# Four batches of attention and a two-stage mixture: the first batch's attention and transform rebuilt, the second batch's queued behind the first unit

## The chip, the cores and the metric

The kernel runs on one NeuronCore of a Trainium2 chip. The metric is device time in microseconds (us): the time of one execution on that core, as a median of three runs.

## The reference, cut to what matters

Three modules in a row, on 4 batches (b) of 576 positions and 512 features (8 heads of 64):

```python
# attention, for each batch and head
qd, kd, vd = mean over groups of 4 positions of q, k, v          # 144 positions
low   = softmax(qd @ kd.T / 8) @ vd, each row repeated 4 times
local = softmax(where(|i - j| < 4, q @ k.T / 8, -1e9)) @ v
x = low + local
# transform, layernorm and MLP
u  = x + real(fft(fft(x, over positions), over features))
x2 = u + relu(layernorm(u) @ w1) @ w2                            # 512 -> 2048 -> 512
# gate, value and output
gate = sigmoid(causal convolution of x2 over 5 positions, one filter per feature)
out  = (gate * (x2 @ w_val)) @ w_out
```

## The kernel before

**Layout.** Activations lie transposed: X is four tiles of 128 features by 584 positions, for one batch. TensorE (PE) multiplies, VectorE (DVE), ScalarE (ACT) and GpSimd (POOL) do the rest, SyncE (SP) issues the loads one behind another (`load`).

**Attention of a batch** (`attn_steps`). The local part goes in five blocks of some 115 query positions, each for two sets of heads (passes): scores dS on PE (L470, L476), their row maximum dmx on DVE, the exponent dP on ACT, row sums dsu and the division on DVE or GpSimd, then transposes dPT (L511) and the values dO (L522), both on PE. The low-resolution part runs beside it: sums over four positions (qkT, L529), scores sc, exponent E, transposes eT, values po (L650) and `base`, which is added to X. For the pooled v (vr) the first batch has six PE products with a matrix of zeros and ones, c_pool; the later batches have adds on GpSimd.

**Transform** (second half of `attn_steps`). Cosines and sines come as products. fs and fF (L698, L706) are sums and differences of X with its mirror image; each of four is split into two fp16 tiles, FH (ACT) and FL (DVE); the products ab of these with `feat` (L729) are split again into AH and AL; their products with `seq` (pp, pq, pn) come back through qs and DS, and are added to X. After it X holds u.

**Layernorm and MLP.** `ln(b, j)` is for a third of a batch (192 positions), a *unit*: sums st by products with ones (L814), squares, rsqrt, and the normalised u. The twelve units run one after another. `mlp_steps` takes a unit through 64 products ph (first matrix), the nonlinearity h and 64 products pc (second one). Unit 0 does this in fp32 on the weights as converted (ph L885, pc L896); the others in three fp16 passes (ph L920, pc L938, three times as many products). `moe2_steps` then does taps (GpSimd, DVE), values (val) and output (out) of the unit.

**Weights.** They come as 64-bit words, in slabs of 1 MB: eight of the first matrix, eight of the second (W2), four of the last two. `to_f32` makes one slab fp32 by three VectorE operations (L261, and two that are recorded at L155). `sumsq_w` forms a gram matrix of the slab on PE, eight products (L306), whose trace gives the scale (`trace_w`) with which `conv_w` splits the slab into two fp16 halves. Two slabs share a ring tile: W_111 in the rows below is the tile of the first two.

**What sets the order.** Every step is put at a position: negative ones come ahead of unit 0, n to n + 1 is unit n (`put`; `spread` lays a list of steps evenly between two positions). The numbers S_*, P_* at the top are these positions. `urgent` raises a kind of step by the offset U, `behind` lets an instruction be issued only after a named one. A scheduler takes the steps in that order on each engine, as far as their inputs allow. Transposes and values (dPT, dO, eT, po, st, val, out) share two PSUM banks, the other results (sc, dS, ab, pp, ...) two more (`TAG`).

Of the kernel before, what the change touches and what calls it, by code (L numbers as in the profile page):

```python
# [1219 lines left out]
```

## Time and profile before

| | us |
|---|---|
| median of 3 runs | 827.89 |
| lowest, highest | 824.13, 828.71 |
| the profiled execution, device time | 826.63 |
| its span in the profile | 824.80 |
| busy: PE, DVE, ACT, POOL | 753.9, 481.0, 397.4, 189.1 |

The mean clock granted to TensorE was 0.935 of full speed. The span is the part of the execution that the profiler sees; 1.83 us lie around it. All durations below are from this one execution. A time in a timeline is counted from the span's start, and W, u, ab and the like are the tiles named above.

### The profile page before, as it was taken

Reading aid. Unit: us, or ns where it says so; the run is one execution under the profiler, and the core shown is the slowest. Engines: PE = TensorE matmul, PEld = TensorE weight load, DVE = VectorE, ACT = ScalarE, POOL = GpSimd, SP = SyncE. Lnnn points to the kernel's source line nnn. Section 1 sums busy time; section 2 is a strip of 40 time slices with the busy share of each in tenths; the row PEclk is TensorE's granted clock in tenths of the full one; section 3 lists DMA queues with packets and bytes.
Section 4 is the critical chain, followed back from the end, with each engine's and each line's share of the span. In section 5 each row is a group of like instructions: output and inputs, shape, how many; then the busy total and the mean of one; then the engine's idle time right before and its main releaser. Section 6 shows DMA issues by size and latency. Waiting matters only on the chain.

```text
span 824.8 us, 17392 instructions
## 1 busy us (share of the span) xinstructions
PE 753.9 (91%) x7234; PEld 651.7 (79%) x7234; DVE 481.0 (58%) x942; ACT 397.4 (48%) x1156; POOL 189.1 (23%) x192
## 2 busy tenths in 40 slices
PE   5887687998979999998989999989989999999996
PEld 2666555887869898886869888978779998989894
DVE  5895968657878575336596732237765526252224
ACT  2573222545674366776562664575552516151512
POOL 0000000015243124363061341341232305040300
PEclk9875666899989999998999999999999999999998
DMA  9753540244202100122021000010110000000001
GB/s 323 312 188 127 182 149 0 86 128 146 77 2 87 59 16 26 35 80 81 29 72 59 1 15 22 9 43 2 53 59 4 14 1 14 14 15 2 26 2 39
DMA packets 25849, 53.58 MB, mean 65 GB/s; under 512 B 1989, under 2 KB 11973, under 8 KB 24746
## 3 DMA queue, kind: packets, MB, share of 16 engines
q1 hardware_dynamic: 25770, 52.47, 18.8%
q8 instruction: 57, 0.93, 0.5%
q14 instruction: 22, 0.18, 0.1%
HBM read 45.37 MB, written 9.45 MB: 66 GB/s over the span
## 4 chain that ended last, share of the span: by engine, by line
PE 65%; DVE 19%; DMA 5%; issue 4%; ACT 4%; POOL 3%; SPq 1%; POOLq 0%; DVEq 0%; ACTq 0%
PE pc L938 18%; PE ph L920 17%; PE val L1017 5%; PE out L1033 4%; DVE W L155 4%; PE dS L476 4%; DVE fF L706 2%; PE dO L522 2%; DVE FL L155 2%; PE ab L729 2%; PE po L650 2%; DMA v<-in_v_dram 2%; PE dPT L511 1%; DMA raw<-in_moe_w_val_dram 1%; DMA raw<-in_moe_w_out_dram 1%
## 5 line engine op out<-in xcount | busy, mean ns | idle before, releaser
L938 PE MATMUL pc<-hh,W 128*128 128x192 f16 x1408 | 199.1, 249 | 1.7 <-ACT hh L924 1.7
L920 PE MATMUL ph<-uh,W 128*128 128x192 f16 x1408 | 195.9, 247 | 0.3 <-ACT uh L849 0.3
L938 PEld LDWEIGHTS <-W 128*128 128x128 f16 x2112 | 178.4, 99 | 16.2 <-issue 11.2
L920 PEld LDWEIGHTS <-W 128*128 128x128 f16 x2112 | 176.0, 98 | 9.0 <-issue 5.7
L938 PE MATMUL pc<-hl,W 128*128 128x192 f16 x704 | 173.8, 250 | 4.3 <-DVE hl L155 4.3
L920 PE MATMUL ph<-ul,W 128*128 128x192 f16 x704 | 173.7, 247 | 1.4 <-DVE ul L850 1.4
L155 DVE SCALAR_TENSOR_TENSOR hl<-ph,hh 128x384 f16<-128x384 f32 x88 | 48.4, 552 | 116.9 <-ACT hh L924 116.9
L161 POOL TENSOR_TENSOR W<-W,tap 128x768 f32<-128x768 f32 x40 | 73.3, 1833 | 164.1 <-ACT tap L996 159.9
L924 ACT ACTIVATE hh<-ph 128x384 f16<-128x384 f32 x88 | 42.2, 484 | 80.7 <-PE ph L920 80.3
L996 ACT ACTIVATE tap<-X,cw 128x192 f32<-128x192 f32 x180 | 66.5, 445 | 8.2 <-DMA out_dram<-osb 4.8
L492 ACT ACTIVATE dP<-dS,dmx 112x128 f32<-112x128 f32 (+2 forms) x160 | 53.2, 372 | 10.2 <-PE dPT L511 9.8
L1017 PE MATMUL val<-yy,W 128*128 128x192 f16 x576 | 54.4, 249 | 2.0 <-DVE yy L155 1.2
L1017 PEld LDWEIGHTS <-W 128*128 128x128 f16 x576 | 49.0, 99 | 5.1 <-issue 3.6
L1033 PE MATMUL out<-W,gh 128*128 128x512 f16 x144 | 46.6, 383 | 0.0
L158 POOL TENSOR_TENSOR dP<-dP,dsu 112x512 f32<-112x512 f32 (+2 forms) x20 | 22.5, 1148 | 72.1 <-DVE dsu L498 57.8
L481 DVE TENSOR_REDUCE dmx<-dS 112x4 f32<-112x512 f32 (+2 forms) x40 | 27.2, 684 | 16.5 <-PE dS L476 16.2
L1033 PE MATMUL out<-W,gl 128*128 128x512 f16 x72 | 27.6, 383 | 2.1 <-DVE gl L155 2.1
L729 PE MATMUL ab<-feat,FH 128*97 128x128 f16 (+5 forms) x192 | 22.0, 244 | 8.1 <-ACT FH L710 7.8
L155 DVE SCALAR_TENSOR_TENSOR W<-W,W 128x1024 int32<-128x1024 int32 x24 | 28.6, 1214 | 0.0
L516 ACT ACTIVATE PT<-dPT 128x448 f32<-128x448 f32 (+2 forms) x40 | 21.7, 558 | 13.3 <-PE dPT L511 13.3
L729 PE MATMUL ab<-feat,FL 128*97 128x128 f16 (+5 forms) x96 | 18.3, 248 | 10.1 <-DVE FL L155 10.0
L511 PE MATMUL dPT<-eye,dP 112*128 112x112 f32 (+2 forms) x160 | 25.2, 294 | 1.6 <-ACT base L654 1.6
(207 smaller groups left out, 1357.8 us busy)
## 6 DMA issues: line engine op xcount, KB each, us to landing
W<-in_moe_w_ch_dram SPq DMA_DIRECT2D x12, 1024.0 KB
X<-in_qk_dram SPq DMA_DIRECT2D x8, 576.0 KB
out_dram<-osb SPq DMA_DIRECT2D x18, 256.0 KB
v<-in_v_dram SPq DMA_DIRECT2D x24, 144.0 KB
vwkv<-in_v_dram SPq DMA_DIRECT2D x12, 256.0 KB
dx<-X SPq DMA_DIRECT2D x4, 576.0 KB
dr<-dx SPq DMA_DIRECT2D x4, 576.0 KB
X<-dr SPq DMA_DIRECT2D x4, 576.0 KB
```

Of the source, the lines that this page charges most:

```text
L155: return eng.scalar_tensor_tensor(out=out, in0=in0, scalar=scalar, in1=in1, op0=op0, op1=op1)
L161: return eng.tensor_tensor(out=out, in0=a, in1=b, op=ALU.add)
L476: T.matmul(out=pss[par][0:nq, a], lhsT=d["X"][row, a, PAD + q0:PAD + q0 + nq], rhs=kT[a // 2][row, a % 2, WIN[r]:WIN[r] + 128], start=Fals ...
L492: A.activation(out=s_[0:nq, a], in_=pss[par][0:nq, a], func=AF.Exp, scale=SCALE, bias=mx[0:nq, par, a:a + 1], **to)
L511: T.transpose(out=ps[:, a, 0:nq], in_=e["s", par][0:nq, a], identity=eye[0:nq, 0:nq])
L729: T.matmul(out=ps[0:n, c0:c1], lhsT=d[x][:, c, sd, e, n0:n0 + n], rhs=feat[:, w, c, c0:c1], start=(t == 0), stop=(t == 5),)
L920: T.matmul(out=ps[:, e], lhsT=w1_ap(pw, kc, 2 * g + e), rhs=uh[px][:, kc, :], start=(t == 0), stop=(t == 11))
L924: A.activation(out=h_, in_=ps, func=AF.Relu)
L938: T.matmul(out=ps[m // 2][:, m % 2], lhsT=w2_ap(pw, kk, m), rhs=x[px][:, e, :], start=(kk == 0 and (pw, px) == (0, 0) and m % 2 == 0), sto ...
L996: A.activation(out=g[:, c], in_=X[:, c, c0:c0 + UT], func=AF.Copy, scale=cw[:, c, t:t + 1])
L1017: T.matmul(out=ps[:, e], lhsT=wv_ap(pw, kc, 2 * mh + e), rhs=m_["y"][px][:, kc, :], start=(t == 0), stop=(t == 11))
L1033: T.matmul(out=ps, lhsT=(gh, gl)[px][:, kc, t * 128:(t + 1) * 128], rhs=wo_ap(pw, kc), start=(n == 0), stop=(n == 11))
```

## The change

- The pooled v of the first batch is added up on GpSimd, by six adds (`pooled_v0`) from eight more loads of v (`load_v4`); c_pool and its products go. The band matrix is loaded first, eye and craw later.
- The gram products of the first matrix (`sumsq_w`) leave the conversions (`w_in`) and come behind the last dO of the first batch (S_G1), those of W2 into unit 0 (S_G2), with W2's scale.
- The first batch's low-resolution steps are dealt out three to a block.
- Its ab products run by quarters (`piece`) into three PSUM banks, one quarter as soon as its FH and FL are there; `sums0` does both channels' pp and pq and then pn.
- The second batch's attention goes from positions -6.4 to -3.8 (P_D) and 0.2 to 1.2 (P_E) to 0.02 to 0.94 and 0.96 to 1.85, its layernorm (P_L) from 1.8 to 2.1. Its dS are issued behind unit 0's first group of ph, as is the sum for unit 1's layernorm, which goes from -6.85 to 0.1 (S_N1). The layernorm of unit 2 is put at 0.9.
- The last four slabs (S_W3) and the last stages of unit 0 (P_T0) come later.

```diff
-LN_V = ((0, 0), (1, 0), (2, 0), (3, 0))
+LN_V = ((0, 0), (0, 2), (1, 0), (2, 0), (3, 0))
...
-S_W3 = (0.945, 1.3)
-P_D = {1: (-6.4, -3.8), 2: (1.6, 3.2), 3: (4.4, 6.0)}
-P_E = {1: (0.2, 1.2), 2: (3.3, 4.5), 3: (6.1, 7.4)}
-P_L = {1: 1.8, 2: 4.9, 3: 7.8}
+S_W3 = (1.02, 1.6)
+S_G1 = (-6.8, -6.7)
+S_G2 = (0.2, 0.44)
+P_D = {1: (0.02, 0.94), 2: (2.0, 3.2), 3: (4.4, 6.0)}
+P_E = {1: (0.96, 1.85), 2: (3.3, 4.5), 3: (6.1, 7.4)}
+P_L = {1: 2.1, 2: 4.9, 3: 7.8}
+P_T0 = ((0.4, 0.75), (0.8, 1.0), (1.3, 1.75))
 EN_G = (1,)
 SUM_V = (0,)
 LN_PE = ((0, 0), (0, 1))
-S_N1 = -6.85
+S_N1 = 0.1
+S_N2 = 0.9
...
-U = {'F': 3000, 'N': 3000, 'X': 600, 'M': 0, 'V': 1000, 'O': 0, 'W': 0, 'R': 2000, 'S': 4000}
+U = {'D': 4000, 'F': 3000, 'N': 3000, 'X': 600, 'M': 0, 'V': 1000, 'O': 0, 'W': 0, 'R': 2000, 'S': 4000}
...
     def load_consts():
-        nc.sync.dma_start(out=eye, in_=c_eye)
-        nc.sync.dma_start(out=craw, in_=conv_t)
-        nc.sync.dma_start(out=sc["pool"], in_=c_pool)
-        nc.sync.dma_start(out=sc["band"], in_=c_band.bitcast(BF16).rearrange("p (a b) -> p a b", a=3))
+        load(out=sc["band"], in_=c_band.bitcast(BF16).rearrange("p (a b) -> p a b", a=3))
+
+    def load_consts1():
+        load(out=eye, in_=c_eye)
 
     def load_consts2():
+        load(out=craw, in_=conv_t)
         load(out=feat, in_=c_feat.rearrange("p (a b c) -> p a b c", a=2, b=2))
         load(out=seq, in_=c_seq.rearrange("p (a b c d) -> p a b c d", a=2, b=3, c=2))
...
         for c in range(8):
             blk = x[:, c * 128:(c + 1) * 128, 1]
-            T.matmul(out=gram[key], lhsT=blk, rhs=blk, start=(first and c == 0), stop=(last and c == 7))
+            behind(st[0]["dO"].ins if i < 8 else None, lambda: T.matmul(
+                out=gram[key], lhsT=blk, rhs=blk, start=(first and c == 0), stop=(last and c == 7)))
...
-        def pooled_v0(vw):
-
-            new_vr()
+        def load_v4():
+
+            t = [pr_t("v4", [QC, 512]) for _ in range(2)] + [acc_t("v4", [QC, 512]) for _ in range(3)]
+            m = mp.tile([QC, 2, 512], F32, tag="M", name="v4")
+            t += [m[:, 0], m[:, 1], startup.tile([QC, 512], F32, name="v4")]
+            d["v4"] = t
+            for n, x in enumerate(t):
+                load(out=x, in_=v4[b, n // 4 * QC:(n // 4 + 1) * QC, n % 4, :])
+
+        def pooled_v0(vw, kc):
+            if kc == 0:
+                new_vr()
+            if kc < 2:
+                x = d["v4"][4 * kc:4 * kc + 4]
+                for o, y, z in ((x[0], x[0], x[1]), (x[2], x[2], x[3]), (d["vr"][:, kc].rearrange("p h d -> p (h d)"), x[0], x[2])):
+                    add(G, o, y, z)
+                return
             gr = pst("cv", [P, P])
-            for kc in range(2):
-                ps = pst("sc", [QC, H * D])
-                rs = (0, 1, 2) if kc == 0 else (2, 3, 4)
-                for r in rs:
-                    n, z = (128 if r == 4 else 112), 72 - 28 * r + 72 * kc
-                    T.matmul(out=ps, lhsT=sc["pool"][0:n, z:z + QC], rhs=vw[r][0:n], start=(r == rs[0]), stop=(r == rs[-1]))
-                A.activation(out=d["vr"][:, kc], in_=ps.rearrange("p (h d) -> p h d", h=H), func=AF.Copy)
...
-                    behind(st[0]["seqed"].ins if b == 1 and r == 0 and par == 0 else None, lambda: T.matmul(
+                    behind(st[0]["ph"].ins if b == 1 and r == 0 else None, lambda: T.matmul(
...
+                ld.insert(4, load_consts1)
                 for r in range(5):
-                    ld.append(lambda r=r: load_vw(r))
+                    ld.insert(5 if r == 0 else len(ld), lambda r=r: load_vw(r))
+                ld.append(load_v4)
                 d["loads"] = [(1.0, f) for f in ld]
-                for z in range(2):
-                    for w in range(2):
-                        steps.append((0.3, lambda z=z, w=w: pool_qk(z, w)))
-                steps.append((0.3, lambda: pooled_v0(vw)))
+                pools = [(0.1, lambda z=z, w=w: pool_qk(z, w)) for w in range(2) for z in range(2)]
...
+                lr = pools[2:] + [(0.1, lambda kc=kc: pooled_v0(vw, kc)) for kc in range(3)] + steps[:]
...
+                if r == 0 and first:
+                    steps.extend(pools[:2])
                 if r > 0:
                     steps.append((1.0, lambda r=r: values(r - 1, es[r - 1])))
                 if r > LR0:
-                    for _ in range(2):
+                    for _ in range(3):
...
+        FC = ((0, 129), (129, 257), (257, 384), (384, 512))
+        abs_ = []
+
+        def piece(c, sd):
+            if not abs_:
+                abs_.extend(pst(x, [97, 512]) for x in ("ab", "ab", "eT"))
+            for i, (n0, n) in enumerate(TT):
+                for e in range(2):
+                    c0, c1 = FC[2 * e + sd]
+                    for x, w in (("FH", 0), ("FH", 1), ("FL", 0)):
+                        T.matmul(
+                            out=abs_[i][0:n, c0:c1], lhsT=d[x][:, c, sd, e, n0:n0 + n], rhs=feat[:, w, c, c0:c1],
+                            start=((c, sd, e, x, w) == (0, 0, 0, "FH", 0)), stop=((c, sd, e, x) == (1, 1, 1, "FL")),
+                        )
...
+        def sums0():
+
+            X, iv = d["X"], d["ivx8"][:, 0:1]
+            a0, a1, b0, b1 = PAD, PAD + HALF, PAD + HALF, PAD + S
+            DSs = []
+            for c in range(2):
+                pp = pst("pp", [P, HALF])
+                pq = pst("pq", [P, HALF])
+                t = 0
+                for i, (n0, n) in enumerate(TT):
+                    for ps, col, j in ((pp, 128 * c, 0), (pq, 258 + 128 * c, 1)):
+                        for q, (x, w) in enumerate((("AH", 0), ("AH", 1), ("AL", 0))):
+                            T.matmul(out=ps, lhsT=d[x][0:n, i, col:col + 128], rhs=seq[0:n, j, i, w, :],
+                                     start=(i == 0 and q == 0), stop=(i == 2 and q == 2))
+                qs = prp.tile([P, HALF], F32, tag="E", name="qs", bufs=3)
+                A.activation(out=qs, in_=pq, func=AF.Copy, scale=iv)
+                DS = prp.tile([P, 2, HALF], F32, tag="E", name="DS", bufs=3)
+                stt(V, DS[:, 0], pp, iv, qs, ALU.mult, ALU.subtract)
+                i = stt(V, DS[:, 1], pp, iv, qs, ALU.mult, ALU.add)
+                gates2.extend([i.ins] * 2)
+                add(V, X[:, c, a0:a1], X[:, c, a0:a1], DS[:, 0])
+                DSs.append(DS)
+            add(V, X[:, 3, a0:a1], X[:, 3, a0:a1], DSs[1][:, 1])
+            pn = pst("pn", [1, HALF])
+            seq_mm(pn, 256, 1, 0)
+            add(V, X[:, 0, b0:b1], X[:, 0, b0:b1], DSs[0][:, 1, HALF - 2:0:-1])
+            for e in (1, 0):
+                A.activation(out=DSs[0][0:1, e], in_=pn, func=AF.Copy, scale=d["ivx8"][0:1, 0:1])
+            add(V, X[:, 2, a0:a1], X[:, 2, a0:a1], DSs[0][:, 1])
+            add(V, X[:, 1, b0:b1], X[:, 1, b0:b1], DSs[1][:, 1, HALF - 2:0:-1])
+            for c in range(2):
+                add(V, X[:, c + 2, b0:b1], X[:, c + 2, b0:b1], DSs[c][:, 0, HALF - 2:0:-1])
+
+        if b == 0:
...
+                    behind(st[0]["ph"].ins if j else None, lambda c=c: T.matmul(
+                        out=ps, lhsT=ones, rhs=src[:, c], start=(c == 0), stop=(c == 3)))
...
+            if g == 0:
+                st[0]["ph"] = i
...
     def w_in(i):
         word_w(i)
-        sumsq_w(i, ("w1", "w2")[i // 8], i % 8 == 0, i % 8 == 7)
...
-    put(S_W1[1], lambda: urgent(w1_scale, "S"))
-    put(S_W2[1], lambda: urgent(w2_scale, "S"))
+    spread([(1.0, lambda i=i: sumsq_w(i, "w1", i == 0, i == 7)) for i in range(8)], *S_G1)
+    put(S_G1[1], lambda: urgent(w1_scale, "S"))
+    spread([(1.0, lambda i=i: sumsq_w(i, "w2", i == 8, i == 15)) for i in range(8, 16)], *S_G2)
+    put(S_G2[1], lambda: urgent(w2_scale, "S"))
...
-            put(n + P_LN if n else S_N1, lambda b=b, j=j: urgent(lambda: ln(b, j + 1), "N"))
+            put((n + P_LN if n > 1 else S_N2) if n else S_N1, lambda b=b, j=j: urgent(lambda: ln(b, j + 1), "N"))
         ps = [P_TAP, P_VAL, P_OUT]
+        if n == 0:
+            ps = list(P_T0)
```

The orders that follow are each engine's instructions before and after, in the program's order; `x4` counts neighbours that read alike.

PE, at the end of the first batch's attention (W_111 to W_114 and W_110 to W_113: the first matrix's slabs; dP of the fourth block, then in the change of the last). Before:

```order
L306 LDWEIGHTS W_114
L306 MATMUL gram<-W_114 128x128
L650 MATMUL po<-ET,vr 64x144 x3
L511 MATMUL dPT<-eye,dP 128x112 x4
L306 LDWEIGHTS W_114
L306 MATMUL gram<-W_114 128x128
...
L511 MATMUL dPT<-eye,dP 128x112 x4
L522 MATMUL dO<-PT,vw_150 64x112
L640 MATMUL eT<-eye,E_596 72x72 x4
```

and in the change:

```order
L665 MATMUL po<-ET,vr 64x144 x4
L523 MATMUL dPT<-eye,dP 128x125 x8
L655 MATMUL eT<-eye,E_605 72x72 x4
L534 MATMUL dO<-PT,vw_149 64x125
L655 MATMUL eT<-eye,E_616 72x72 x4
L534 MATMUL dO<-PT,vw_149 64x125 x7
L310 LDWEIGHTS W_110
L310 MATMUL gram<-W_110 128x128
```

All 64 gram products of the first matrix now stand behind the last dO, where 64 stood between the blocks' transposes and values before.

DVE, in the first batch's transform (s_x: its scale; W_115 and W_114: the tile of the first two W2 slabs; W_119, W_120, W_118: raw words). Before:

```order
L161 TENSOR_TENSOR X<-X,base 128x576 x4
L698 TENSOR_TENSOR fs<-X 128x577 x3
L706 TENSOR_TENSOR fF<-fs 128x289 x6
L698 TENSOR_TENSOR fs<-X 128x577
L155 SCALAR_TENSOR_TENSOR FL<-fF,s_x_492,FH 128x2x289
L261 TENSOR_SCALAR W_115<-W_119 128x1024
L155 SCALAR_TENSOR_TENSOR FL<-fF,s_x_492,FH 128x2x289
L261 TENSOR_SCALAR W_115<-W_120 128x1024
L155 SCALAR_TENSOR_TENSOR FL<-fF,s_x_492,FH 128x2x289
L706 TENSOR_TENSOR fF<-fs 128x289 x2
L155 SCALAR_TENSOR_TENSOR W_115<-W_119,W_115 128x1024
L155 SCALAR_TENSOR_TENSOR W_115<-W_120,W_115 128x1024
```

and in the change:

```order
L164 TENSOR_TENSOR X<-X,base 128x576 x4
L161 TENSOR_TENSOR tr<-gram,eye 128x128
L317 TENSOR_REDUCE ss_w_1111<-tr 128x1
L728 TENSOR_TENSOR fs<-X 128x577 x3
L736 TENSOR_TENSOR fF<-fs 128x289 x6
L728 TENSOR_TENSOR fs<-X 128x577
L158 SCALAR_TENSOR_TENSOR FL<-fF,s_x_558,FH 128x2x289 x3
L736 TENSOR_TENSOR fF<-fs 128x289 x2
L158 SCALAR_TENSOR_TENSOR FL<-fF,s_x_558,FH 128x2x289
L158 SCALAR_TENSOR_TENSOR AL<-ab,AH 97x258
L265 TENSOR_SCALAR W_114<-W_118 128x1024
```

Four conversion operations of W2 leave the FL and stand behind the first AL; the trace of the first matrix's gram comes ahead of fs.

PE, ahead of unit 0's first product ph (dS, dPT, dO: the second batch's; W_117, W_118: W2's last four slabs; W_111 and W_110: the first matrix). Before:

```order
L814 MATMUL st<-sq,ones 128x192 x4
L511 MATMUL dPT<-eye,dP_1281 128x115 x4
L470 LDWEIGHTS bandb
L470 MATMUL dS<-bandb 112x512
L476 MATMUL dS<-X 112x128 x4
L511 MATMUL dPT<-eye,dP_1286 128x115 x4
L522 MATMUL dO<-PT,vwq 64x115 x8
L306 LDWEIGHTS W_117
L306 MATMUL gram<-W_117 128x128
...
L306 MATMUL gram<-W_118 128x128
L885 MATMUL ph<-u_1086,W_111 128x192
```

and in the change (W_115: two W2 slabs):

```order
L310 LDWEIGHTS W_115
L310 MATMUL gram<-W_115 128x128
L880 MATMUL st<-X,ones 128x192 x3
L880 MATMUL st<-sq,ones 128x192 x4
L952 MATMUL ph<-u_1004,W_110 128x192
L952 MATMUL ph<-u_1004,W_111 128x192
L952 MATMUL ph<-u_1004,W_112 128x192
L952 MATMUL ph<-u_1004,W_113 128x192
...
L880 MATMUL st<-X,ones 128x192 x4
L482 LDWEIGHTS bandb
L482 MATMUL dS<-bandb 115x512
```

Of the second batch's products none stands ahead of ph any more, and of W2's grams none directly; a first sum for unit 1 and the second batch's scores follow the first group of ph.

## Rows read from the trace of the kernel before

**Rows 1.** The page's part 1: busy us, share and instructions of each engine.

```profile
PE 753.9 (91%) x7234; PEld 651.7 (79%) x7234; DVE 481.0 (58%) x942; ACT 397.4 (48%) x1156; POOL 189.1 (23%) x192
```

**Rows 2.** Stages: busy us of each engine (count), then granted clock, DMA share, GB/s.

```profile
20.00:30.00 10.00, 10.00 (x92) 7.29 (x90) 7.50 (x14) 5.01 (x20) 0.11 (x1) 1.00 1.01 420
60.00:80.50 20.50, 18.31 (x118) 13.77 (x118) 11.64 (x29) 9.87 (x27) 0.00 (x0) 0.58 0.33 106
80.50:115.40 34.90, 22.74 (x173) 16.89 (x173) 29.38 (x52) 7.06 (x15) 0.59 (x6) 0.67 0.48 172
115.40:132.20 16.80, 12.51 (x53) 10.29 (x53) 11.41 (x23) 5.55 (x27) 0.00 (x0) 0.70 0.23 79
132.20:146.75 14.55, 9.95 (x57) 7.68 (x58) 14.55 (x19) 5.61 (x21) 1.58 (x2) 0.57 0.15 42
146.75:220.30 73.55, 69.31 (x452) 61.35 (x451) 48.29 (x105) 39.57 (x116) 16.76 (x18) 0.95 0.35 107
220.30:824.80 604.50, 576.22 (x6097) 511.81 (x6094) 318.13 (x621) 301.33 (x846) 169.56 (x157) 0.98 0.10 31
```

**Rows 3.** The chain that ended last, to 160 us: start, us, what.

```profile
61.26 1.82 PE gram L306 x16
...
81.22 1.42 DVE fs L698 x2
...
86.27 0.60 DVE W L261
...
89.67 2.27 DVE W L155 x2
...
92.73 2.92 PE ab L729 x25
...
115.39 1.20 DVE dmx L481 x2
...
121.81 1.98 PE dS L476 x8
...
131.24 0.97 DVE u L158
...
136.75 14.78 issue
```

**Rows 4.** PE's timeline, 72 to 157 us: start, us, what, idle before.

```profile
72.23 1.93 PE L511 MATMUL dPT<-eye,dP 125*128 125x125 f32 x8
...
146.75 5.09 PE L885 MATMUL ph<-u,W 128*128 128x192 f32 x16
...
153.66 2.87 PE L885 MATMUL ph<-u,W 128*128 128x192 f32 x16 [0.58 <-ACT h L887]
```

**Rows 5.** VectorE's timeline, 64 to 139 us.

```profile
64.42 1.29 DVE L158 TENSOR_TENSOR dP<-dP,dsu 125x512 f32<-125x512 f32 x2
...
101.06 0.41 DVE L155 SCALAR_TENSOR_TENSOR AL<-ab,AH 96x256 f16<-96x256 f32 x1
...
133.99 5.13 DVE L529 TENSOR_REDUCE qkT<-X 128x288 f32<-128x1152 f32 x4
```

**Rows 6.** GpSimd's instructions by shape over the span: busy us, mean ns, idle before.

```profile
L158 POOL TENSOR_TENSOR dP<-dP,dsu 112x512 f32<-112x512 f32 x12 | 13.1, 1113 | 31.9 <-DVE dsu L498 22.1 <-PE dPT L511 9.8
...
L161 POOL TENSOR_TENSOR vr<-v 72x256 f32<-72x256 f32 x12 | 9.2, 769 | 33.5 <-DMA v<-in_v_dram 32.9 <-PE dS L476 0.6
```

**Rows 7.** VectorE's timeline, 195 to 201 us.

```profile
195.63 1.21 DVE L155 SCALAR_TENSOR_TENSOR W<-raw,W 128x512 int32<-128x512 int32 x1
...
199.44 0.68 DVE L155 SCALAR_TENSOR_TENSOR W<-raw,W 128x512 int32<-128x512 int32 x1
```

**Rows 8.** PE's timeline, first and last of the second batch's three last head pairs.

```profile
198.86 0.71 PE L604 MATMUL sc<-qkT 64*72 64x144 f32 x4 [1.30 <-ACT E L618]
...
246.44 0.93 PE L650 MATMUL po<-ET,vr 72*64 72x144 f32 x6
```

**Rows 9.** The chain that ended last, one run of fp16 products.

```profile
652.49 1.98 PE pc L938 x24
```

More of the change, by code (lines that the diff above doesn't have):

```diff
@@ L71 @@
 P_LN = 0.3
-D1_H = 3
+D1_H = 0
 LN_H = ()
@@ L112, in constants, with attn_moe_kernel @@
         "c_eye": eye,
-        "c_pool": (np.arange(160)[None, :] == 72 + np.arange(128)[:, None] // 4).astype(np.float32),
     }
 @with_exitstack
-def attn_moe_kernel(ctx, tc, qk_t, v_t, w1, w2, w_val, conv_t, w_out, c_feat, c_seq, c_band, c_eye, c_pool, out):
+def attn_moe_kernel(ctx, tc, qk_t, v_t, w1, w2, w_val, conv_t, w_out, c_feat, c_seq, c_band, c_eye, out):
     nc = tc.nc
@@ L521, in values @@
                         h = 2 * a + par
-                        T.matmul(out=po[par * 64:par * 64 + 64, a, 0:nq], lhsT=vw[r][:, h * D:(h + 1) * D],
-                                 rhs=pts[par][:, a, 0:nq], start=True, stop=True)
+                        d["dO"] = T.matmul(out=po[par * 64:par * 64 + 64, a, 0:nq], lhsT=vw[r][:, h * D:(h + 1) * D],
+                                           rhs=pts[par][:, a, 0:nq], start=True, stop=True)
                 A.activation(out=d["X"][:, :, PAD + q0:PAD + q0 + nq], in_=po[:, :, 0:nq], func=AF.Copy)
@@ L558, in dense @@
                 for z in range(2):
-                    for w in range(2):
+                    for w in range(1 if b == 1 else 2):
                         steps.append((0.1, lambda z=z, w=w: pool_qk(z, w)))
+                if b == 1:
+                    v1 += [(0.1, lambda z=z: pool_qk(z, 1)) for z in range(2)]
             lr = []
@@ L566, in dense @@
                 lowres()
-                lr = steps[:]
+                lr = pools[2:] + [(0.1, lambda kc=kc: pooled_v0(vw, kc)) for kc in range(3)] + steps[:]
                 steps[:] = low
@@ L710, in f @@
                     A.activation(out=h_, in_=F, func=AF.Copy, scale=d["sx"][:, 0:1])
-                    i = stt(V, d["FL"][:, c, sd, :, 0:HALF], F, d["sx"][:, 0:1], h_, ALU.mult, ALU.subtract)
+                    stt(V, d["FL"][:, c, sd, :, 0:HALF], F, d["sx"][:, 0:1], h_, ALU.mult, ALU.subtract)
                     if b == 0:
-                        gates2.extend([i.ins] * 2)
+                        piece(c, sd)
                 steps.append((2.1, f))
@@ L723, in f @@
             def f(i=i, n0=n0, n=n):
-                ps = pst("ab", [97, 512])
-                for (c0, c1), sd, e in (((0, 129), 0, 0), ((129, 257), 1, 0), ((257, 384), 0, 1), ((384, 512), 1, 1)):
+                ps = abs_[i] if b == 0 else pst("ab", [97, 512])
+                for (c0, c1), sd, e in () if b == 0 else [(FC[z], z % 2, z // 2) for z in range(4)]:
                     t = 0
@@ L758, in seq_mm @@
                     t += 1
-        for c in range(2):
+        def sums0():
[30 more added lines that the diff above has]
+        if b == 0:
+            steps.append((3.0, sums0))
+        for c in range(2 if b else 0):
             def f(c=c):
@@ L789, in attn_steps @@
         if b == 0:
+            steps[:n_chain] = [(c, lambda f=f: urgent(f, "D")) for c, f in steps[:n_chain]]
             d["cuts"] = [d["turned"], n_chain]
@@ L813, in colsum @@
                 for c in range(4):
-                    T.matmul(out=ps, lhsT=ones, rhs=src[:, c], start=(c == 0), stop=(c == 3))
+                    behind(st[0]["ph"].ins if j else None, lambda c=c: T.matmul(
+                        out=ps, lhsT=ones, rhs=src[:, c], start=(c == 0), stop=(c == 3)))
                 return ps
@@ L884, in h_group @@
                     o = (m % 8) * 128
-                    T.matmul(out=ps[:, e], lhsT=W[kc * 2 + m // 8 + 1][:, o:o + 128], rhs=u()[:, kc, :],
-                             start=(kc == 0), stop=(kc == 3))
+                    i = T.matmul(out=ps[:, e], lhsT=W[kc * 2 + m // 8 + 1][:, o:o + 128], rhs=u()[:, kc, :],
+                                 start=(kc == 0), stop=(kc == 3))
+            if g == 0:
+                st[0]["ph"] = i
             A.activation(out=hs[-1][:, g % 2], in_=ps, func=AF.Relu)
@@ L1085, in w_in2 @@
             load_w(i)
-        w_in(i)
+        word_w(i)
     def w_in(i):
         word_w(i)
-        sumsq_w(i, ("w1", "w2")[i // 8], i % 8 == 0, i % 8 == 7)
     def w_out_(i):
```

2 lines of the change are left out of this document (1 added, 1 removed).

## The prediction

> **What bounds the kernel now.** The page comes first: TensorE (PE) is busy for 753.9 of 824.8 us [rows 1], so no other engine can be worth much over the whole span. The stages [rows 2] say where PE isn't the bound. From 220.3 us to the end it is busy 576.2 of 604.5 us at a granted clock of 0.98. Ahead of 146.75 us it is another kernel: VectorE (DVE) is busy 29.4 of 34.9 us in the first batch's transform and all 14.55 us of the stretch ahead of unit 0, while PE is granted only 0.57 to 0.70 of its clock. There the chain that ended last is to be read [rows 3]: it runs through weight conversions (W), the transform (fs, ab, X), the layernorm (u) and 14.78 us that belong to no work on the path. PE's own timeline shows what unit 0 waits for: its first product, ph, starts at 146.75 [rows 4], though its input u is done at 132.2 (131.24 + 0.97) [rows 3]. In PE's queue 16 gram products of W2 slabs stand in front of it, and those slabs are converted by DVE behind 5.13 us of sums for the second batch [rows 5]. So up to 146.75 the kernel is a chain of small latencies, after it a queue of PE work. A gain in front is kept only as far as PE's work isn't moved behind.
>
> **The change, part by part.** Steps are counted from the event named in front of them; all go against the profiled execution (span 824.8, device time 826.63, which is 1.26 below the median of three).
>
> *1. The first batch's attention, up to fs (81.22 [rows 3]).* The six pooling products of v leave PE and become six adds on GpSimd. No row has their shape (72x512). From below, such an add is the 0.77 us of a 72x256; from above 1.11 us of a 112x512 [rows 6]; I take 1.1, being as wide, so 6.6 us on an engine that is idle there. They need eight more loads of v, 1.18 MB, which stand on SP's queue in front of the weights. At the 420 GB/s of the stretch 20 to 30 us [rows 2] they delay W1 by 2.8 us. W1's first conversion now stands behind the second mask's maximum on DVE, so that hides the delay; uncovered it would cost those 2.8. GpSimd's adds do reach DVE: beside such an add a conversion of a raw half took 1.21 us, and 0.68 us without one [rows 7]. With 0.53 us for each of six, DVE, which bounds this stretch, loses 3 us. The Trainium skill ("SBUF — State Buffer", "Who interferes with whom") speaks harder against the move: a VectorE op with two SBUF inputs and a GpSimd op that reads SBUF exclude each other for the whole instruction. By it the loss would be all 6.6 us and the sum 3.6 us worse; the row shows the half of it.
>
> DVE's other work up to the fifth block's normalisation (64.42 + 1.29 = 65.7 [rows 5]) is the same. It starts its maxima about 2 us sooner. So this point stays where it is, within 2 us. From there to fs it takes 15.5 us now. All 64 gram products of W1 now come after the last dO (the first fence above), and DVE's fs stands behind the trace of that gram. At the low clock 16 of them took 1.82 us [rows 3], so 64 take 7.3; 24 of them now stand in PE's queue ahead of the last block, so 40 more cost 4.5 us. Against it, the fourth block, which comes to PE only behind those 24, is through by then (its transposes dPT and dO are some 4 us at this clock, by 1.93 for a dPT [rows 4]), and w1's scale with its split leaves the stretch. The three nearly cancel, and with DVE's 2 us in front I take fs 2 us sooner. Ends: 8 us sooner if PE is at full clock and GpSimd costs nothing, 3 us later if neither.
>
> *2. fs to the last FL (81.22 to 92.7): −3.5.* Two conversions of 0.60 and two of 1.13 (2.27) stand between the FL of before [rows 3]; after, none (second fence).
>
> *3. Last FL to last AL (92.73 to 101.47 [rows 3, 5]): −2.* The products ab now run quarter by quarter behind each FH and FL, into three PSUM banks at once, and all but 12 are done by the last FL. What stays: 12 products, some 1.4; an evacuation, 0.4; six AL of 0.41 [rows 5] and three conversions among them (0.60, 1.13, 0.60): 6.7 of 8.7 us.
>
> *4. Last AL to X (115.39): −1, between −4 and +1.* The same 45 products and DVE's 10 ops; the nine pn products go behind both channels, but the last X needs pn. At the clock of before little is won.
>
> *5. X to u (115.39 to 132.2): −7.9.* Between them DVE's maxima (1.20) and PE's dS of the second batch (1.98 for one pass of two in a block) stand on the chain [rows 3], from 115.39 to 123.79; of this only layernorm's own 1.9 us (subtract and square) must stay; then some 1.5 us of unit 1's layernorm and a maximum among the rsqrt steps. After, the second batch's dS and unit 1's layernorm stand behind unit 0's first group. Bounds −6 to −9.
>
> *6. u to ph: −14.5.* Ph follows the squares' sums at once (third fence).
>
> The front sums to −30.9: ph at about 116. What was in it doesn't vanish. *7. +14, from 10 to 17.* Between 115.4 and 146.75 PE was busy 12.51 + 9.95 us [rows 2]; at its 0.70 and 0.57 that is 14.4 us of full clock, of which some 2 are layernorm's of unit 0; the second batch's first dS (two passes at once, another 1.98 at most) and the grams that now follow (36 of W2 against 8, at 0.08) make it 14 again. They now stand in unit 0's queue, where PE is the bound: one of two passes of a dS was 1.98 us at the low clock [rows 3], half of it at the full one. *8. Second batch's later chain: +2, from 0 to 8.* Its low-resolution attention leaves unit 0 for unit 1; the PE work is only moved, and 4.2 us of waits (73.55 − 69.31 [rows 2]) go along. But its transform now ends just ahead of unit 3: the sums of the layernorm stand right in front of the first ph of that unit, with some 12 us of other products (out, val, dS, dPT) put in the gap. I take 2 us that they don't fill. Conversions of W2 that were done ahead of u (5 slabs of 8, now 2.5) cost nothing as long as PE has ph and dS to do: a rival, below.
>
> Sum: −30.9 + 14 + 2 = −14.9, 826.6 − 14.9 = 811.7; say **811 us**.
>
> **Rivals.**
> *A: the wait goes into unit 0.* DVE has 5.5 slabs left at u (2.9 us each by 0.60 + 2 x 1.13: 16 us), the 5.13 of the second batch's sums [rows 5] and some 9 of its maxima and normalisations: 30 us. PE has 48 of its 64 ph products, dS and the rest, 37 us, in front of the last 16 grams. 7 us of slack speak against it; for it, that slabs 14 and 15 load only into buffers that 11 and 12 leave. If the loads come 15 us late, unit 0 stands 8 us: 819.
> *B: the clock is released sooner.* In the attention's end it was granted 0.58, in the transform 0.67 [rows 2]. The 64 grams now form one run, and the ab products follow each other more closely. At full clock ph's 16 records take 2.87 instead of 5.09 us [rows 4]; step 1 would then give −6, step 4 −3 and the start of unit 0 −2: some 8 us more, 803. Against: PE idles during fs and fF as before. The Trainium skill's rule ("TensorE: Matmul & The Clock Gate", "What's actually happening") is that the low clock is the default and sustained activity releases it; the stretches of rows 2 agree, idle ones low, and by it B would come true as far as the run of grams is unbroken.
> *C, on the other side: the second batch's low-resolution chain is late.* Its last three head pairs now ran from 198.86 to 247.3 [rows 8], 48.5 us, with eT waiting for GpSimd. After, they stand between 0.57 and 1.09 of unit 1's products in PE's queue: with 0.0825 us a product (1.98 for 24 [rows 9]) 16.5 us, with at most 12 for their own products (sc 0.71, po 0.93 [rows 8]) and others between some 28 us. If their pace stays that of before, PE stands 20 us: 832, slower. It decides once these waits exceed 15 us. For it: GpSimd has unit 0's taps between the v adds there, and v's loads stand behind raw weights on SP. Against: part of the 48.5 is PE's own work of unit 0.
> *D: nothing is won.* All ends of step 1 and 4 go wrong and A costs its 8: 826.
>
> **How the numbers follow.** Forecast 0.53 (804 to 817), A 0.17, B 0.12, D 0.10, C 0.08. The range 798 to 824 takes in A, B and the most of the forecast's bounds; left out are C, half of D and the lowest ends. A change under 0.5% (4 us) can't be told from none, the runs of before lying 4.6 us apart. Faster takes the forecast, A, B and a little of D: 0.84; within 0.5% most of D: 0.09; slower C: 0.07.
>
> **What would show it.** Right: fs at 76 to 82; four FL in a row and AL done within 7 us; u at 110 to 121 with ph at its heels; unit 0's end (first ph of fp16 products, now 220.3) at 190 to 198; from there to the end some 612 us. Wrong: grams with idle PE in front in unit 0 (A), eT and po waiting in unit 1 over 15 us (C), or fs after 84. The prediction fails in size if moved work costs other than 14 us.

## The result, and the profile after

| | before | after |
|---|---|---|
| median, us | 827.72 (4 runs) | 814.56 (4 runs, 811.96 to 818.39) |
| ratio, 95% interval | | 0.9867 (0.9828 to 0.9906) |
| profiled execution, span | 826.63, 824.80 | 818.39, 816.60 |

The forecast was 811, 798 to 824. A second set of the same kernel (experiment 5) gave 812.26. Its executions lie up to 10 us apart (803.9 to 814.5), so one profile is read for its order and its waits, and times of 3 us are compared by medians alone. The profiled execution, 818.39, is the slowest of its four.

The stages of the changed kernel, cut at the events that the prediction counts by (fs, X, the first ph, unit 1); columns as in [rows 2]:

```profile
20.00:60.00 40.00, 38.34 (x183) 28.21 (x181) 39.97 (x79) 22.60 (x86) 6.39 (x6) 1.00 0.67 261
60.00:81.90 21.90, 19.28 (x160) 14.86 (x160) 10.76 (x27) 10.19 (x31) 0.00 (x0) 1.00 0.64 213
81.90:108.66 26.76, 16.81 (x145) 12.72 (x146) 23.70 (x47) 6.85 (x14) 2.39 (x7) 0.87 0.43 153
108.66:118.51 9.85, 3.53 (x12) 2.73 (x11) 7.28 (x23) 1.88 (x2) 0.00 (x0) 0.53 0.12 47
118.51:190.38 71.87, 71.87 (x516) 65.59 (x517) 59.27 (x101) 39.57 (x122) 1.11 (x2) 0.97 0.27 93
190.38:816.60 626.22, 589.04 (x6161) 520.16 (x6159) 332.51 (x665) 311.17 (x888) 181.04 (x170) 0.97 0.11 37
```

To be seen: unit 0 now has no idle time on TensorE (71.87 of 71.87 us), and the stretch behind it is longer than before, 626.22 against 604.50 us [rows 2], with 589.04 us busy against 576.22. Of the 29.9 us by which unit 1 starts sooner, 21.7 are lost again there.

VectorE's timeline holds the front's events. First the start of fs before, then the changed kernel:

```profile
80.54 2.10 DVE L698 TENSOR_TENSOR fs<-X 128x577 f32<-128x577 f32 x3 [0.28 <-ACT X L679]
```

```profile
81.89 2.09 DVE L728 TENSOR_TENSOR fs<-X 128x577 f32<-128x577 f32 x3
...
86.79 2.28 DVE L158 SCALAR_TENSOR_TENSOR FL<-fF,s_x,FH 128x578 f16<-128x578 f32 x3
...
90.66 0.82 DVE L158 SCALAR_TENSOR_TENSOR FL<-fF,s_x,FH 128x578 f16<-128x578 f32 x1 [0.85 <-ACT FH L740]
...
97.71 0.41 DVE L158 SCALAR_TENSOR_TENSOR AL<-eT,AH 96x256 f16<-96x256 f32 x1
...
107.85 0.81 DVE L164 TENSOR_TENSOR X<-X,DS 128x289 f32<-128x289 f32 x2
...
117.50 0.96 DVE L161 TENSOR_TENSOR u<-uc,r 128x768 f32<-128x768 f32 x1
```

And TensorE's timeline at unit 0's first product and at unit 1's:

```profile
118.51 4.99 PE L952 MATMUL ph<-u,W 128*128 128x192 f32 x16 [4.39 <-DVE u L161]
...
190.38 0.26 PE L989 MATMUL ph<-uh,W 128*128 128x192 f16 x1
```

Ph starts 0.05 us behind u (14.55 before), three FL stand in a row, and unit 1 starts 29.9 us sooner (190.38 against 220.3). The span is only 8.2 us shorter, and the median 13.2.

### The profile page after: what moved, and what is told of

Same layout as the page of the kernel before. It is cut to its first block, busy times and chain, and to the rows that moved or that the text cites. A ratio compares the mean times of both kernels' runs of the same rounds, so it can differ in the third digit from the quotient of the medians.

```text
span 816.6 us, 17405 instructions
## 1 busy us (share of the span) xinstructions
PE 748.7 (92%) x7222; PEld 651.0 (80%) x7222; DVE 482.3 (59%) x946; ACT 396.8 (49%) x1154; POOL 193.7 (24%) x194
## 4 chain that ended last, share of the span: by engine, by line
PE 69%; DVE 16%; DMA 8%; ACT 3%; issue 2%; POOL 2%; SPq 0%; ACTq 0%; POOLq 0%; DVEq 0%
PE pc L1007 18%; PE ph L989 17%; PE dS L488 5%; PE out L1102 4%; PE val L1086 4%; DVE W L158 4%; PE ph L952 3%; PE dO L534 3%; DVE fF L736 2%; DMA v<-in_v_dram 2%; PE po L665 2%; DMA W<-in_moe_w_ch_dram 2%; PE dPT L523 2%; PE pc L965 1%; PE eT L655 1%
## 5 line engine op out<-in xcount | busy, mean ns | idle before, releaser
L989 PE MATMUL ph<-uh,W 128*128 128x192 f16 x1408 | 198.7, 248 | 0.3 <-ACT uh L916 0.3
L164 POOL TENSOR_TENSOR W<-W,tap 128x768 f32<-128x768 f32 x40 | 75.2, 1879 | 152.6 <-ACT tap L1065 123.3
L493 DVE TENSOR_REDUCE dmx<-dS 112x4 f32<-112x512 f32 (+2 forms) x40 | 27.0, 683 | 13.2 <-PE dS L488 12.8
L952 PE MATMUL ph<-u,W 128*128 128x192 f32 x128 | 24.7, 350 | 4.4 <-DVE u L161 4.4
L952 PEld LDWEIGHTS ph<-u,W 128*128 128x128 f32 x128 | 22.8, 206 | 5.2 <-DVE u L161 4.9
L1102 PEld LDWEIGHTS <-gh 128*128 128x128 f16 x144 | 14.4, 101 | 15.5 <-issue 2.1
```

The source lines that it names most:

```text
L164: return eng.tensor_tensor(out=out, in0=a, in1=b, op=ALU.add)
L952: i = T.matmul(out=ps[:, e], lhsT=W[kc * 2 + m // 8 + 1][:, o:o + 128], rhs=u()[:, kc, :], start=(kc == 0), stop=(kc == 3))
L989: T.matmul(out=ps[:, e], lhsT=w1_ap(pw, kc, 2 * g + e), rhs=uh[px][:, kc, :], start=(t == 0), stop=(t == 11))
L1102: T.matmul(out=ps, lhsT=(gh, gl)[px][:, kc, t * 128:(t + 1) * 128], rhs=wo_ap(pw, kc), start=(n == 0), stop=(n == 11))
```

## The experiments

Each kernel was timed beside the kernel before on the same chip; the ratios are to that.

**1. The rebuild alone.** Positions (P_D, P_E, P_L, S_N1, S_W3), gates, W2's grams and unit 0's last stages as before; only the first batch stays rebuilt.

```diff
-P_D = {1: (0.02, 0.94), 2: (2.0, 3.2), ...
+P_D = {1: (-6.4, -3.8), 2: (1.6, 3.2), ...
-behind(st[0]["ph"].ins if b == 1 and r == 0 ...
+behind(st[0]["seqed"].ins if b == 1 and r == 0 and par == 0 ...
```

> The changed kernel with the second batch (its attention, unit 1's and unit 2's layernorm, the W2 grams, the last slabs and unit 0's last stages) put back where it was before; only the first batch's rebuild stays. Theory (ledger): the changed kernel's rows give the rebuild 0.7 - 2.7 - 1.4 - 3.4 = -6.8 us up to X, and these stay: X done at about 109, ph at about 140, 821 us (818 to 823). Rival (VectorE's sum): the W2 conversions that were moved behind AL must still be done ahead of the first ph, VectorE has the same work in front of ph as before, so ph stays at 144 to 147 and the time at 825 to 829 although X is done 7 us sooner.

829.87 us, 1.0062 (1.0036 to 1.0088): nearly the rival's time (825 to 829), not by the rival's way. Ph was early, at 115.69, and not at 144. But the second batch was not back in its old place: with the rebuilt front the scheduler put its first scores behind half of unit 0. TensorE's timeline:

```profile
148.32 0.28 PE L224 MATMUL tot<-ss_w,ones 128*128 128x1 f32 x2
148.46 0.41 PE L479 MATMUL dS<-bandb 128*115 128x512 bf16 x1
```

Its stages from the first ph to 200 us, to 300 us, and to the end, and under them the same for the changed kernel:

```profile
115.69:200.00 84.31, 83.53 (x654) 76.62 (x655) 65.16 (x99) 48.75 (x137) 10.83 (x8) 0.98 0.23 76
200.00:300.00 100.00, 79.30 (x688) 64.12 (x685) 62.95 (x153) 38.19 (x119) 28.21 (x36) 0.78 0.28 88
300.00:827.30 527.30, 503.21 (x5332) 446.61 (x5330) 263.00 (x510) 263.83 (x756) 147.05 (x133) 0.99 0.08 28
```

```profile
200.00:300.00 100.00, 90.49 (x963) 79.65 (x961) 70.64 (x156) 50.48 (x134) 35.72 (x38) 0.97 0.25 78
```

Scores that start 24 us later than in the changed kernel (124.64) go with 20.7 us of idle time on TensorE between 200 and 300 us (9.5 in the changed kernel), at a granted clock of 0.78. Most of it is spent on steps of the second batch's chain: eT 7.0 us, ab 6.0, st 3.7, sc 2.0.

```profile
PE eT L652 <- POOL E L158: 7.0, 4, 3.5
```

The early ph was worth nothing here; by these waits, what it is worth depends on that chain. Why the scheduler places it so stays open, and so does the price of the rebuild alone, with the second batch in its old place.

**2. The move alone.** The kernel before with the second batch's positions and gates, W2's grams, the last slabs and unit 0's last stages of the change.

> The kernel before with only the second batch moved behind unit 0's first group (positions, gates, W2 grams, last slabs, last stages as in the change); the first batch is as before. Theory (ledger): u and ph come 7.0 + 14.5 us sooner, the moved work and its waits cost 20.0 us: 826 us (822 to 829), ph at about 125. Rival (the move is what pays, the rebuild was eaten): 816 to 820 us. Second rival (W2's conversions, which now come later by none, make unit 0's last products wait): over 830.

840.65 us, 1.0173 (1.0121 to 1.0225). Slower, outside the theory's 822 to 829; the second rival's time (over 830), but not its place, as TensorE is idle for 2.0 us of unit 0's 72.9. Ph came at 129.0, 17.7 us sooner than before, and unit 1 at 201.9, 18.4 us sooner; all of it and more was given back behind. TensorE's waits between 110 and 400 us (engine, who waits, for whom: us in total, times, longest):

```profile
PE pc L945 <- DVE hl L159: 12.4, 4, 3.4
PE ph L890 <- DVE u L162: 4.4, 1, 4.4
PE st L818 <- DVE X L165: 3.1, 1, 3.1
```

In the kernel before the waits for hl are 1.5 us there, in the changed kernel 6.9. This profile is the longest of the kernel's six executions (846.8), so its waits are read for their order only. As built in experiments 1 and 2, rebuild and move lose 3 and 14 us apart and win 13 together: their terms are not prices that add up.

**3. v pooled on TensorE again.** The six products and c_pool are back, the eight loads and six adds of GpSimd are gone.

> The changed kernel with the first batch's v pooled by the six products on TensorE again, without the eight more loads and the six GpSimd adds. Theory (clock): those products were what kept TensorE busy from 12.9 to 20.9 us before, and without them it stays at the lower of its levels until 74 us; with them the eight dS products of a block take 1.1 us again from about 21 us on instead of 2.05, for a part of the attention at least; fs starts 2 to 6 us sooner and the time is 809 to 813. Rival (VectorE and GpSimd): dS stay at 2.05 us, VectorE gains the 3 us that the adds cost it between 20 and 27 us, fs 3 us sooner. Second rival (attention bound by VectorE's own work): fs within 1 us, 814 to 815; the products cost what the adds cost.

812.75 us, 0.9852 (0.9815 to 0.9889): no difference from the changed kernel. The clock theory is right on the rows: its TensorE timeline has

```profile
12.17 4.44 PE L420 MATMUL sc<-vw,pool 112*72 112x512 f32 x6 [1.22 <-DMA vw<-in_v_dram]
16.75 1.12 PE L483 MATMUL dS<-kTa,X 64*112 64x128 f32 x8
...
31.02 1.12 PE L483 MATMUL dS<-kTa,X 64*112 64x128 f32 x8
32.42 1.93 PE L483 MATMUL dS<-kTa,X 64*112 64x128 f32 x8
```

where the changed kernel has 2.04 us at 17.11. But the higher level hardly shortens the attention: from the first maximum to the end of the fifth block's normalisation it took 53.4 us (54.6 in the changed kernel, 53.1 before). Fs came at 74.7, sooner as forecast, because the first maximum came 3.4 us sooner (9.04 for 12.45) and the tail behind the normalisation was 2.5 us shorter; the end did not move with it. The products are 8.35 us of TensorE's own work (1.97, 4.44 and 1.94).

**4 and 8. Unused products in TensorE's first wait** (24 of a constant into an unused bank; in 8, 12 more behind the first scores). They compute nothing that is used.

```diff
+with tc.high_priority(offset=9000):
+    warm(24)            # T.matmul(out=t, lhsT=ones, rhs=ones, ...)
```

> The changed kernel with 24 products of the constant ones by itself into an unused bank, issued first, while TensorE waits for the first loads; they compute nothing that is used. Theory (clock): TensorE is at the higher level when the scores start at 9.6 us, dS take 1.1 us for eight for as long as it stays busy, and fs starts 2 to 8 us sooner: 806 to 812. If the idle 2 to 3 us behind the first scores bring the level down again, dS of the second block take 2.05 and nothing is won. Rival (attention bound by VectorE): dS at 1.1 us through blocks 2 to 4 and fs still at 81 to 82: 814.

> The changed kernel with the 24 unused products at the start, and 12 more behind the first scores, where TensorE waits for v. Theory (clock): dS at 1.1 us for eight as far as 30 us, as where v was pooled on TensorE, and fs 2 to 5 us sooner than in the changed kernel; time 2 to 5 us lower. Rival (VectorE bounds the attention, and the level falls again by 35 us anyway): fs within 1.5 us, time within 1.5 us.

818.32 us, 0.9911 (0.9876 to 0.9946), and 814.06, 0.9879 (0.9827 to 0.9931). Nothing won: the second block's dS are at the lower level again (from 18.78 us eight took 2.05 us; in experiment 8 eight took 2.04 at 18.04), fs at 80.3 and 80.4. Whether a high level held through the attention would help isn't shown.

**5. The changed kernel again.**

> The changed kernel itself, so that the runs sent with it can be compared with it on the same chip. 812 to 819 us. If its first score products of eight again take 2.05 us between 20 and 70 us, the low level in the attention belongs to the kernel and not to one profile.

812.26 us, 0.9815 (0.9772 to 0.9858). Eight dS again took 2.04 to 2.05 us up to 40 us: the low level belongs to the kernel. Fs at 77.8 in this one, since the loads came 1.7 us sooner and the tail of the attention was 2.2 us shorter.

**6. The last four slabs later.** `S_W3 = (1.2, 1.75)` in place of `(1.02, 1.6)`.

> The changed kernel with the last four slabs' conversions at positions 1.2 to 1.75 in place of 1.02 to 1.6. Theory (waits in unit 1): VectorE stands in its queue for raw words that come only when the second batch's values leave their buffers, with unit 1's fp16 remainders hl behind it: PE waited 6.9 us for hl. Later, the words are there: hl waits fall under 3 us and the time by 2 to 5 us against the changed kernel. Rival (the waits only move): the second batch's low-resolution steps, which are then beside the conversions, lose as much: within 1.5 us.

817.56 us, 0.9888 (0.985 to 0.9926). Not confirmed: the longest wait for hl stayed at 4.5 us, since the words of the third slab stood at the same place in VectorE's order. The rival's 1.5 us is not met either; against experiment 5 the time is 5.3 us up, against the first set 3. Why it rose isn't shown.

**7. ab in whole banks.** The first batch's ab products as before, behind the last FL.

> The changed kernel with the first batch's ab products as before, a whole PSUM bank after the last FL in place of quarters. Theory (step 3): 2 to 4 us between the last FL and the last AL come back, ph 2 to 4 us later, and as PE idles there, the time rises by 2 to 4 us against the changed kernel. Rival: the conversions of W2 fill VectorE in that gap, so ph is later but unit 0 has less to wait for: within 1 us.

818.56 us, 0.9904 (0.9871 to 0.9938), 4 to 6 us above the changed kernel. From the last FL (ends at 92.97) to the last AL (103.08) it took 10.1 us instead of 6.6: the 3.5 us of step 3 by themselves.

**9. Unit 0's tap sums on VectorE.** The one line of `conv` that adds up the taps:

```diff
-                add(G, m_["g"], m_["g"], g)
+                add(V if i == 0 else G, m_["g"], m_["g"], g)
```

> The changed kernel with the four tap sums of unit 0 on VectorE in place of GpSimd. Theory (contention): in unit 1 a half of a slab's conversion took 2.32 to 2.98 us beside GpSimd's adds and 0.68 without, and unit 1's remainder hl stood behind it; the tap sums cost VectorE 4 us of its own, and the longest wait for hl falls from 4.5 to about 3 us (what is left is VectorE's wait for the raw words, 2.8 us); time 0 to 3 us lower than the changed kernel's 812 to 815. Rival (the words are what is waited for): the longest wait for hl stays over 4, and the time is the same or 1 to 3 us higher for the added VectorE work.

799.52 us, 0.9692 (0.9642 to 0.9742): 13 us below the changed kernel's second set and 15 below its first, four times the most that was expected. In the changed kernel, VectorE's timeline of unit 1 and GpSimd's beside it:

```profile
203.16 0.43 DVE L265 TENSOR_SCALAR W<-raw 128x512 int32<-128x512 int32 x1 [2.81 <-DMA raw<-in_moe_w_out_dram]
203.51 1.28 DVE L158 SCALAR_TENSOR_TENSOR W<-W,s_w,W 128x1024 f16<-128x1024 f32 x1
204.70 2.98 DVE L158 SCALAR_TENSOR_TENSOR W<-raw,W 128x512 int32<-128x512 int32 x1
207.61 0.54 DVE L158 SCALAR_TENSOR_TENSOR hl<-ph,hh 128x384 f16<-128x384 f32 x1
...
203.99 1.37 POOL L164 TENSOR_TENSOR vr<-v 72x256 f32<-72x256 f32 x1 [1.92 <-DMA v<-in_v_dram]
205.33 1.80 POOL L164 TENSOR_TENSOR tap<-tap 128x768 f32<-128x768 f32 x1
```

The conversion that is 0.68 us alone was issued at 204.70, while GpSimd added for vr, and ended at 207.68, 0.55 us behind the tap sum (207.13): it was held for the rest of one add and for the whole of the next. Behind it stood hl, and behind hl TensorE:

```profile
208.20 0.32 PE L1007 MATMUL pc<-hl,W 128*128 128x192 f16 x1 [4.54 <-DVE hl L158]
```

Not all of the 4.54 us is GpSimd's doing, since VectorE had waited for raw words until 203.16. TensorE's waits for hl between 180 and 320 us, in the changed kernel (5.7 us in experiment 5) and with the taps moved:

```profile
PE pc L1007 <- DVE hl L158: 6.9, 5, 4.5
```

```profile
PE pc L1007 <- DVE hl L158: 0.7, 1, 0.7
```

The same groups of VectorE's instructions from unit 1's start to 232 us (count, busy us, mean ns, idle before), first of the changed kernel, then with the taps moved:

```profile
L158 DVE SCALAR_TENSOR_TENSOR W<-raw,W 128x512 int32<-128x512 int32 x11 | 14.0, 1276 | 0.0
```

```profile
L158 DVE SCALAR_TENSOR_TENSOR W<-raw,W 128x512 int32<-128x512 int32 x14 | 10.1, 730 | 0.0
L164 DVE TENSOR_TENSOR tap<-tap 128x768 f32<-128x768 f32 x4 | 4.3, 1081 | 0.0
```

Four sums cost VectorE 4.3 us, and 14 halves took 10.1 us where 11 had taken 14.0. The second batch's low-resolution chain, which goes through the same queue, was done sooner: its last `X<-X,base` started 59.8 us behind unit 1's first product instead of 68.1. From 220 to 350 us, with taps on VectorE and in the changed kernel:

```profile
220.00:350.00 130.00, 129.51 (x1352) 111.12 (x1350) 74.41 (x175) 74.90 (x237) 41.80 (x47) 1.00 0.17 54
```

```profile
220.00:350.00 130.00, 123.10 (x1228) 104.02 (x1226) 81.58 (x185) 72.31 (x233) 42.31 (x46) 0.96 0.16 50
```

6.4 us of idle time are gone, and in the same stretch TensorE got through 1352 products instead of 1228, at a granted clock of 1.00 instead of 0.96. It repeats: TensorE is busy for 123.62 us of that stretch in experiment 5, and for 129.77 in experiment 12, which has the taps on VectorE too.

A rival is GpSimd's own queue, where the second batch's sums for v stand between the taps. It isn't what held the last of them, for GpSimd was idle ahead of these:

```profile
218.89 0.88 POOL L164 TENSOR_TENSOR ptv<-v 72x256 f32<-72x256 f32 x1 [8.87 <-PE ph L989]
```

In experiment 5 the same wait (8.30 us) is put down to the loads of v. Those stand on SP, whose waits from 206 to 214 us in the changed kernel are put down to VectorE's conversions (7.7 and 1.4 us). No run parts the two ways, though, and the edit also let the scheduler put the second hl of unit 1 ahead of the conversion that it had stood behind.

The rule that the prediction weighed (the Trainium skill, "SBUF — State Buffer", "Who interferes with whom": both engines shut each other out for the whole instruction) is what the row at 204.70 shows, 2.98 us for 0.68.

**10. The first matrix's grams back with the conversions.** `sumsq_w` in `w_in`, w1's scale at S_W1.

> The changed kernel with the first matrix's 64 gram products back with their slabs' conversions, ahead of and between the values of the first batch. Theory (step 1): behind the last dO they cost about what they cost between the blocks: fs within 2 us, time within 2 us of 812 to 815. Rival (the run of grams holds the last base sums and the trace up): without it fs is 3 to 4 us sooner and the time 2 to 4 us lower. Second rival (grams in the attention slow the values): fs 2 to 4 us later, time 2 to 4 us higher.

812.78 us, 0.9847 (0.981 to 0.9884): the same time, as the theory said. Fs came at 75.38, sooner as the rival said (77.80 in experiment 5, 81.89 in the first set); the end did not move.

**11. The second batch a quarter of a unit later.** P_D (0.3, 1.1), P_E (1.12, 1.95), P_L 2.15 for it.

> The changed kernel with the second batch's attention later by a quarter of a unit (0.3 to 1.1 and 1.12 to 1.95, its layernorm at 2.15). Theory (its chain is what the move is paid with): PE waits for its low-resolution steps and its transform in units 1 to 3, as it did where the scores came 30 us late with the old positions: 3 to 10 us higher than 812 to 815. Rival (PE has other work there): within 2 us.

815.79 us, 0.9893 (0.9851 to 0.9936): 1.2 and 3.5 us above the two sets of the changed kernel. Inconclusive. The first scores came at 129.81 us (124.64 in the changed kernel), and TensorE stayed busy in unit 0 (66.53 of 66.53 us). Experiment 1, with scores 24 us later, is 15 us above the changed kernel; that its other edits have no part in that isn't shown.

**12. Both: v on TensorE, taps on VectorE.**

> The changed kernel with the first batch's v pooled on TensorE again and unit 0's tap sums on VectorE: both of GpSimd's adds that stood beside VectorE's conversions are gone. Theory: the two gains add: 808 to 812. Rival (the products cost TensorE as much as VectorE gains, and the taps are VectorE's own work): 812 to 815, as the changed kernel.

799.62 us, 0.9685 (0.9645 to 0.9725): the taps' gain, and nothing on top of it. Experiments 9 and 12 beat both kernels.

## Why the prediction was right

It was right in time, sign and in most of its terms; by the profiled executions (repeated: experiment 5's, 809.00 us):

| step | forecast | measured | repeated | from |
|---|---|---|---|---|
| 1 up to fs | -2 | +1.35 | -2.7 | 80.54 to 81.89 |
| 2 to last FL | -3.5 | -2.55 | -2.6 | 9.59 for 12.14 |
| 3 to last AL | -2 | -2.15 | -2.6 | 6.64 for 8.79 |
| 4 to X | -1 | -3.4 | -3.4 | 10.54 for 13.92 |
| 5 to u | -7.9 | -7.0 | -6.6 | 9.80 for 16.81 |
| 6 to ph | -14.5 | -14.5 | -14.5 | 0.05 for 14.55 |
| 7 moved PE work | +14 | +15.4 | +13.9 | busy from ph to the end, 660.91 for 645.53 |
| 8 waits behind ph | +2 | +4.7 | +0.9 | idle there, 37.18 for 32.52 |
| sum | -14.9 | -8.2 | -17.6 | |

Steps 2 to 6 repeat within 0.5 us; 1, 7 and 8 differ by 1.5 to 4.1 us from one execution to the next, and the forecast lies between the two sums. That the median came as near as 3 us to 811.7 is in part luck: step 4 won more than forecast, steps 2 and 5 less.

**Steps 5 to 7** came within 1.5 us. The parts named for step 7 (14.4 less 2, about 1 for a pass of dS, 28 grams at 0.08) come to 15.6 and not to 14. Experiment 7 isolates step 3. In step 2 the last FL waited 0.85 us for its FH.

**Step 1**, by the two executions, came 3.4 us worse than forecast and 0.7 better. GpSimd's adds cost about their price. VectorE's instructions beside them in the changed kernel:

```profile
20.74 1.79 DVE L161 TENSOR_TENSOR dP<-dP,dsu 115x512 f32<-115x512 f32 x1
22.45 1.22 DVE L637 TENSOR_SCALAR lsu<-lsu 72x2 f32<-72x2 f32 x1
23.59 0.68 DVE L161 TENSOR_TENSOR dP<-dP,dsu 115x512 f32<-115x512 f32 x1
...
20.71 1.26 POOL L164 TENSOR_TENSOR v<-v,v 72x512 f32<-72x512 f32 x1 [0.43 <-DMA v<-in_v_dram]
22.33 1.32 POOL L164 TENSOR_TENSOR v<-v,v 72x512 f32<-72x512 f32 x1 [0.35 <-DMA v<-in_v_dram]
```

A normalisation took 1.79 instead of 0.68, a small step of the low-resolution sums (lsu) 1.22 instead of 0.15, two conversions (at 24.86 and 26.24) 1.1 us more together, another small step (dsu at 19.80) 0.35 more: some 3.6 us by 3 forecast; the six adds took 8.6 us instead of 6.6. The row from which the price was taken isn't half of a lock, as the prediction read it. The add beside that conversion was GpSimd's

```profile
194.59 1.70 POOL L161 TENSOR_TENSOR ptv<-v 72x256 f32<-72x256 f32 x1
```

which had 0.66 us to go when the conversion was issued at 195.63; the conversion ended 0.55 us behind it, at 196.84. The normalisation at 20.74 ended 0.56 us behind an add too (22.53 for 21.97). So what one meeting costs goes by how much of the add is left.

What the forecast missed is that the six products taken from TensorE had been what preceded its higher level. Without them eight dS take 2.04 us from 17 us on, where they took 1.12 at 21 and 28 us before, and the products stay there until the run of grams at 74 to 81 us. Before, then in the change:

```profile
21.02 1.12 PE L476 MATMUL dS<-kTa,X 64*112 64x128 f32 x8
```

```profile
17.11 2.04 PE L488 MATMUL dS<-kTa,X 64*112 64x128 f32 x8
```

So in step 1 rival B came the other way round. It cost little, as experiment 3 shows: VectorE, busy for 39.97 of the 40 us from 20 to 60, sets this stretch. Nor did an earlier fs move the end there or in experiment 10 (7.2 and 6.5 us sooner than in the first set, 3.1 and 2.4 sooner than in experiment 5). In step 4 rival B's time came, -3.4 for -3, and its sign: two pp products took 0.41 us at 100 us, and 0.69 at 106.5 us before. The prediction also read the stages before as agreeing with the clock rule, the idle ones low; the one from 60 to 80.5 us doesn't, busy for 18.31 of 20.50 us at 0.58.

**Step 8** held its range (0 to 8); its size can't be told from the two executions. Rival A (waits in unit 0) didn't come: unit 0 has none, 4.2 us less than before. They did go along, as forecast: of the 58.12 us behind unit 1's start TensorE is idle for 10.6 (10.0 repeated), where it was for 5.2. From there to the end it idles 3.5 us more (0.4 repeated) for the 2 forecast. Rival C's sign, eT and po waiting, came with 1.9 us of eT only; what unit 1 waits for is hl, and experiment 9 shows what that hangs on. The prediction named the taps beside the v adds on GpSimd under rival C and gave the case 0.08. It didn't see that VectorE, and hl with it, would stand behind both.

**The split between the units** was wrong: 612 us were forecast from unit 1 to the end, and it took 626.22 (621.4 repeated); unit 0, from ph to unit 1, got 1.7 us shorter (71.87 for 73.55), with 516 products for 452; what was put into it pushed other work behind it.

**The reading as a sum** failed under test. The terms hold for the change as a whole. In experiments 1 and 2 ph came 31 and 18 us sooner, and the time rose by 3 and 14. By experiment 1's waits the second batch's chain then decides, not ph; for experiment 2 the cause stays open.

## What to carry to other kernels

Where one engine is the bound behind a slow front, count what the front's gain does to that engine's idle time to the end of the program: here 28 us sooner became 13 in the median (8 in the profiled execution). Look at which engine another one locks out, not only at which is busy: moving four additions from a half-idle GpSimd to VectorE won 13 us, about as much as the whole change had. And test the parts together as well as alone.

## What the runs showed of the hardware that had not been expected

- A VectorE instruction of 0.68 us took up to 2.98 beside GpSimd's adds; a TENSOR_SCALAR on 72x2 elements took 1.22 for 0.15. A TENSOR_REDUCE beside such an add (dmx at 19.19, 0.69 us) was not held.
- The granted clock of the stages can be off. In the changed kernel's profile 20 to 60 us reads 1.00, while eight dS take 2.04 to 2.05 us there, as they do in the kernel before at 36 us and in experiment 4, whose same stretch reads 0.54. Durations of one shape were compared instead.
- Executions of the changed kernel on one chip differ by up to 10.6 us (803.92 to 814.48); in its two profiles 4 us of 9 lie ahead of the first ph.
